# The old scores' bank booked one access at a time, attention's outputs loaded by pairs of token tiles, and a new list of due-time shifts, in a planned kernel of attention and a Fourier mix

## The chip, the cores and the metric

The kernel runs on one core of a Trainium2 chip. The metric is the device time of one execution in microseconds (us). Before the change it is 1681.3 us, the median of three runs (1677.09 to 1683.54).

The engines are TensorE (PE; PEld is its load of weights), VectorE (DVE), ScalarE (ACT) and GpSimd (POOL). SyncE (SP) issues the DMAs. PSUM, into which TensorE writes, is used in banks of 512 float32 numbers per partition.

## The reference

Two independent layers are computed and set side by side: attention over a window of 256 tokens (S = 2048, D = 1024, 32 heads of 32), and the real part of a two-dimensional Fourier transform, written as products with matrices.

```python
qkv = (x @ wqkv).reshape(B, S, 3, H, Dh)            # q, k, v by head
scores = einsum("bhqd,bhkd->bhqk", q, k) * Dh ** -0.5
mask = (i - j >= 0) & (i - j < 256)
p = softmax(where(mask, scores, -1e9))
a = einsum("bhqk,bhkd->bhqd", p, v) -> (B, S, D) @ wo

a_ = x @ dft_hid_re.T ; b_ = x @ dft_hid_im.T
b = dft_seq_re @ a_ - dft_seq_im @ b_
return concatenate([a, b], axis=-1)
```

## The kernel before

**Numbers.** Inputs are float32. Each operand is scaled by a power of two and split into a high and a low float16 part (ACT writes the high one, L503, L504 and L1201; DVE the low one, L508, L511 and L1202). A product is three TensorE passes: high by high, high by low, low by high (`PASSES`). The scale comes from the largest magnitude in the operand: a reduction (L529 on DVE, L1070 on ACT), a transpose of the column of maxima by TensorE into the bank `old` (L543, L1160), a reduction there (L545, L1162), and three tiny DVE instructions.

**Products.** Most large products take seven block products in place of eight (`seven`); the sums of blocks that this needs run on POOL and DVE (L1177). `seven` uses four PSUM banks `m`. Its first product is copied by ACT into a second bank as a start value (L1288), then accumulated into in both. Results are evacuated by ACT (L1379, L1572) and DVE (L1382, L1575).

**Stages.** To about 250 us: q, k and v. From there to about 1565 us attention runs block by block beside further products: the rest of q, k and v, then the Fourier layer, whose unit is `x` (the hidden transform) or `c` (the one along the sequence). Last come eight pairs of token tiles of the product with `wo`.

**A block of attention** is 128 queries of two heads. `s_step` writes the scores of the last two key tiles into a bank `s` and those of the third, oldest tile into one half of the bank `old` (L653). A DVE copy under a mask takes the old scores into the place of those above the diagonal (L664). DVE finds the maxima (L669), ACT the bias (L673) and the two exponentials, one for each head (L679). ACT and DVE split the result (L504, L508), a DMA transposes it (L688), POOL masks it (L694, L697). `v_step` multiplies two blocks by v into the one bank `pv` (L730), and DVE normalises (L735, L737, L741). `o_step` stores an output of four heads, transposed, in `ots`, by chunk of 512 tokens, group of four heads, part and token.

**The end.** `o_load` brings attention's outputs back, two loads for each pair of token tiles. `o_blocks` adds high and low parts (L1550), makes four sums (L1177), and splits them.

**What sets the order.** Nothing is issued as the Python code runs. `op` records every operation with its engine, an assumed duration, and what it reads and writes. `Plan.close` gives each a due time, counted back from TensorE's order of products. `Plan.run` moves due times: each entry of `SHIFTS` names a stretch of 20 us and a seed, and all operations due in that stretch are moved by pseudo-random amounts. `Plan.forward` then walks through time with the assumed durations: an engine that comes free takes the ready operation with the earliest due time. The order found there is written out as fixed instruction queues. On the chip each engine runs its queue in order and waits on semaphores. These waits follow from the tiles that instructions touch, whatever the plan assumed.

A `Ring` is a set of buffers used in turn. One with `free=True` gives a slot to whoever asks, once its last user is done. The bank `old` is such a ring with two slots, its two halves, shared by the old scores and the transposes of maxima.

Of the kernel before, what the change touches and what calls it, by code (L numbers as in the profile page):

```python
# [12 lines left out]
F16 = mybir.dt.float16  # L13
# [7 lines left out]
P = 128  # L21
# [64 lines left out]
class Ring:  # L86

    def __init__(self, plan, make, n, free=False):
        self.make, self.n, self.free, self.bufs, self.after = make, n, free, [], None
        plan.rings.append(self)  # L90
# [24 lines left out]
def scatter(n, seed):  # L115
# [6 lines left out]
SHIFTS = (  # L122
# [16 lines left out]
)  # L139


class Plan:
# [79 lines left out]
    def forward(self):  # L222
# [5 lines left out]
        held = {}  # L228
        gate = {}
        for ring in self.rings:  # L230
            if ring.free:
                for b in ring.bufs:
                    for o in b.heads:
                        gate.setdefault(o, []).append(b)
                    for o in b.ops:
                        held.setdefault(o, []).append(b)
                    b.todo, b.has = len(b.ops), False
# [16 lines left out]
        def start(o, t, e):  # L254
            nonlocal bus
            cost = o.cost
# [9 lines left out]
            if o.dma:  # L266
                bus = max(bus, fin - (BETWEEN if e == "SP" else 0.0)) + o.dma[0]
                fin = bus + o.dma[1]
                if e == "SP":
                    lanes.append(fin)  # L270
            fin += DRAIN if e == "PE" else SEM
            o.at, o.fin = t, fin
            order.append(o)
# [10 lines left out]
        def pick(e, t):  # L284
# [4 lines left out]
            while h:  # L289
# [6 lines left out]
                if any(not b.has and not room[b.ring] for b in gate.get(o, ())):  # L296
                    skipped.append(item)
                    continue
                got = o
                break  # L300
            for item in skipped:
                heapq.heappush(h, item)
            if got is not None and e == "DVE" and got.port:
                wait = lock["POOL"] - t - SHARED[e]
                if wait > 0.05:
                    skipped = []
                    while h and len(skipped) < 12:
                        item = heapq.heappop(h)
                        o = item[2]
                        skipped.append(item)  # L310
                        if not o.port and o.cost < wait + SLIP and not any(not b.has and not room[b.ring] for b in gate.get(o, ())):
                            skipped.pop()
                            skipped.append((got.due, got.n, got))
                            got = o
                            break
# [87 lines left out]
def fused_kernel(ctx: ExitStack, tc: tile.TileContext, xa, wqk, wv, xb, wd, cs, out):  # L403
# [56 lines left out]
    old_bank = ps_v.tile([P, 2, 2 * P], F32, name="old")  # L460
    old_ring = Ring(R, lambda k: old_bank[:, k], 2, free=True)
    s_ring = Ring(R, lambda k: ps_s.tile([P, 2, 2 * P], F32, tag="s", name=f"s_{k}"), 2)
# [77 lines left out]
    def scale_of(key, v, s, wk, down=2.0 ** -14, loose=False):  # L540
# [10 lines left out]

        dve(0.47, rest, w=[wk])

# [15 lines left out]
    def dkey(*a):  # L569
        return ("dram", *a)  # L570
# [25 lines left out]
    def attention():  # L596
# [33 lines left out]
        def s_step(b):  # L630
# [47 lines left out]
            for h in range(2):  # L678
                op("ACT", 0.32 + 0.00085 * w, lambda h=h: nc.scalar.activation(  # L679
                    sv()[:, h], sv()[:, h], AF.Exp, bias=bias.t[:, h:h + 1], scale=es),  # L680
                   r=[bias, ("esc", g // 2)], w=[(S, h)])
            hl = hl_ring.new()
# [468 lines left out]
    def u_look(n):  # L1151
# [18 lines left out]

        dve(0.7, rest, r=[("fa", p)], w=[v, f])
        su[n], fu[n] = v, f
# [361 lines left out]
    def o_load(q):  # L1534
        if q < NT // 2:
            for t in (2 * q, 2 * q + 1):
                b = os_[t] = raw_ring.new()
                load(lambda b=b: b.t.bitcast(F16).rearrange("p (g h t) -> p g h t", g=NG, h=2),
                     lambda t=t: ots[t // 4, :, :, :, t % 4 * P:t % 4 * P + P], 740, [b],
                     r=[dkey("o", t // 4, g) for g in range(NG)])  # L1540

    def o_blocks(q):
# [3 lines left out]
        r1, r2 = (y_ring if q == 0 else late_ring).new(), (y_ring if q == 0 else late_ring).new()  # L1546
        tv = lambda b: b.t.bitcast(F16).rearrange("p (g h t) -> p g h t", g=NG, h=2)
        ov = lambda b, h: b.t.bitcast(F16).rearrange("p (a g h t) -> p a g h t", a=2, h=2, t=P)[:, :, :, h]
        for r, o in ((r1, o1), (r2, o2)):
            dve(1.22, lambda r=r, o=o: nc.vector.tensor_tensor(r.t.rearrange("p a (g t) -> p a g t", t=P), ov(o, 0),  # L1550
                                                               ov(o, 1), op=ALU.add), r=[o], w=[(r, 0), (r, 1)],
                port=True)
        H_ = lambda r, a: (lambda: r.t[:, a])
        summed("DVE", H_(r1, 0), H_(r1, 0), H_(r2, 0), 512, [(r2, 0)], [(r1, 0)])
        summed("DVE", H_(r2, 0), H_(r2, 0), H_(r2, 1), 512, [(r2, 1)], [(r2, 0)], False)
        summed("DVE", H_(r2, 1), H_(r2, 1), H_(r1, 0), 512, [(r1, 0)], [(r2, 1)])
        summed("DVE", H_(r1, 1), H_(r1, 1), H_(r2, 1), 512, [(r2, 1)], [(r1, 1)])
        us = {}
        for r, pair in ((r2, (4, 2)), (r1, (1, 6))):
            x, y, ap = duo()  # L1560
# [3 lines left out]
            us[pair[0]], us[pair[1]] = position(x), position(y)  # L1564
        whole = lambda o, k: (lambda h, d: ((lambda: tv(o)[:, HG * k + d, h]), o))
        oq[q] = (whole(o1, 0), us[1], us[2], whole(o1, 1), us[4], whole(o2, 1), us[6])

    def pair_of_tiles(q, lhs, rhs, y1, y2, f, fk, out_y, hook, more=False, order=ORDER):
        half = lambda y, e: y.t[:, e] if len(y.t.shape) == 3 else y.t[:, e * CH:(e + 1) * CH]

        def copy(y, e, ps):
            op("ACT", 0.6, lambda: nc.scalar.activation(half(y, e), ps.t, AF.Copy, scale=f()), r=[ps, *fk], w=[(y, e)])  # L1572

# [182 lines left out]
```

## Time and profile before

| | us |
|---|---|
| median of three runs | 1681.3 |
| the profiled execution | 1678.3 |
| its span in the profile | 1676.4 |
| TensorE busy | 1647.7 |
| VectorE busy | 1400.5 |
| ScalarE busy | 1153.4 |
| GpSimd busy | 813.4 |

The profile is of one execution. "Idle before" a group of instructions is the time its engine stood still ahead of them, put down to the event that came last. Rows of products on TensorE overlap, since a product's row ends when its last result is written, well after the next has begun; so TensorE's busy time is the time in which any product is in flight. A list of waits has, for each pair of waiting and awaited lines, the total, the number of times and the longest. Rows of the timeline have the start, the time from the first start to the last end of the merged instructions, their count, and the idle time ahead.

### The profile page before, as it was taken

Reading aid. Unit: us, or ns where it says so; the run is one execution under the profiler, and the core shown is the slowest. Engines: PE = TensorE matmul, PEld = TensorE weight load, DVE = VectorE, ACT = ScalarE, POOL = GpSimd, SP = SyncE. Lnnn points to the kernel's source line nnn. Section 1 sums busy time; section 2 is a strip of 40 time slices with the busy share of each in tenths; the row PEclk is TensorE's granted clock in tenths of the full one; section 3 lists DMA queues with packets and bytes.
Section 4 is the critical chain, followed back from the end, with each engine's and each line's share of the span. In section 5 each row is a group of like instructions: output and inputs, shape, how many; then the busy total and the mean of one; then the engine's idle time right before and its main releaser. Section 6 shows DMA issues by size and latency. Waiting matters only on the chain.

```text
span 1676.4 us, 31757 instructions
## 1 busy us (share of the span) xinstructions
PE 1647.7 (98%) x11413; PEld 889.2 (53%) x11413; DVE 1400.5 (84%) x2376; ACT 1153.4 (69%) x1988; POOL 813.4 (49%) x797
## 2 busy tenths in 40 slices
PE   9999999999999999999999999999999999999999
PEld 4446787675444555555445545545555555554444
DVE  7989997667999998778999986898885799999651
ACT  6656636666987988977977766877665777775231
POOL 0233401323776954447956774754544476773100
PEclk9999999999999999999999999999999999999999
DMA  7389799979999889899899999789999779999732
GB/s 282 130 316 360 246 332 288 283 163 221 251 264 289 221 195 281 220 288 257 189 231 273 262 289 294 183 198 255 253 242 259 169 176 271 273 289 233 155 94 76
DMA packets 470302, 400.33 MB, mean 239 GB/s; under 512 B 342016, under 2 KB 397056, under 8 KB 470144
## 3 DMA queue, kind: packets, MB, share of 16 engines
q1 hardware_dynamic: 470144, 398.30, 90.0%
q8 instruction: 89, 1.46, 0.4%
q14 instruction: 69, 0.57, 0.1%
HBM read 215.37 MB, written 109.45 MB: 194 GB/s over the span
## 4 chain that ended last, share of the span: by engine, by line
PE 59%; DVE 17%; DMA 8%; ACT 7%; issue 6%; POOL 3%; SPq 0%; DVEq 0%; POOLq 0%; ACTq 0%
PE m L788 53%; DMA raw<-in_cs_dram 3%; DVE sth L1202 3%; DVE hl L508 3%; PE pv L730 3%; DMA t<-hl 2%; DVE mx L669 2%; PE s L653 2%; DVE s L664 2%; DVE ybig L1575 2%; ACT s L679 1%; ACT sth L1201 1%; ACT hl L504 1%; DVE reg L508 1%; POOL raw L1177 1%
## 5 line engine op out<-in xcount | busy, mean ns | idle before, releaser
L788 PE MATMUL m<-reg,sth 128*128 128x512 f16 x4992 | 1150.8, 379 | 10.8 <-DVE sth L1202 2.3
L788 PEld LDWEIGHTS <-sth 128*128 128x128 f16 x5748 | 544.7, 97 | 598.1 <-issue 12.3
L694 POOL TENSOR_SCALAR_AFFINE_SELECT z<-t 128x512 f16<-128x512 f16 x224 | 181.6, 821 | 373.9 <-PE pv L730 185.1
L1177 POOL TENSOR_TENSOR raw<-raw,raw 128x512 f32<-128x512 f32 x176 | 257.1, 1463 | 207.7 <-DVE sth L1202 164.7
L679 ACT ACTIVATE s<-s,bias,escs 128x256 f32<-128x256 f32 (+1 forms) x512 | 269.1, 528 | 12.3
L508 DVE TENSOR_TENSOR hl<-s,hl 128x512 f16<-128x512 f32 (+1 forms) x256 | 170.4, 668 | 65.0 <-ACT hl L504 62.4
L673 ACT ACTIVATE bias<-mx,pshift,escs 128x2 f32<-128x2 f32 x256 | 97.6, 383 | 159.4 <-DVE mx L669 158.7
L697 POOL TENSOR_SCALAR_AFFINE_SELECT t<-t 128x512 f16<-128x512 f16 x224 | 185.9, 841 | 5.3
L669 DVE TENSOR_REDUCE mx<-s 128x2 f32<-128x512 f32 (+1 forms) x256 | 169.0, 665 | 1.6
L1202 DVE SCALAR_TENSOR_TENSOR sth<-raw,sc,sth 128x1024 f16<-128x1024 f32 (+1 forms) x128 | 158.1, 1239 | 11.9 <-ACT sth L1201 11.5
L504 ACT ACTIVATE hl<-s 128x512 f16<-128x512 f32 (+1 forms) x256 | 147.5, 579 | 4.5 <-DMA t<-hl 1.4
L1201 ACT ACTIVATE sth<-raw,sc 128x1024 f16<-128x1024 f32 (+1 forms) x128 | 131.0, 1035 | 13.1 <-POOL raw L1177 6.5
L653 PEld LDWEIGHTS <-qk 96*128 96x128 f16 x1056 | 92.2, 98 | 83.5 <-issue 8.5
L1177 POOL TENSOR_TENSOR raw<-raw 128x512 f32<-128x512 f32 x80 | 119.9, 1500 | 31.3 <-DVE reg L511 20.9
L664 DVE COPY_PREDICATED s<-upper,old 128x256 f32<-128x256 uint32 x224 | 93.3, 420 | 19.7 <-PE s L653 8.8
L788 PE MATMUL m<-xz,sth 128*128 128x512 f16 x492 | 108.9, 379 | 0.0
L1070 ACT ACTIVATE junk<-raw 128x1024 uint8<-128x1024 f32 x82 | 86.5, 1054 | 25.4 <-DMA raw<-in_cs_dram 22.1
L730 PE MATMUL pv<-vt,t 128*128 128x65 f16 x1984 | 100.6, 185 | 0.0
L730 PEld LDWEIGHTS <-t 128*128 128x128 f16 x1984 | 89.1, 96 | 20.3 <-issue 8.8
L653 PE MATMUL s<-qk,qk 96*128 96x128 f16 (+1 forms) x608 | 94.5, 252 | 2.8 <-DVE hl L508 2.0
L730 PE MATMUL pv<-vt,z 128*128 128x65 f16 (+1 forms) x896 | 89.8, 185 | 5.5 <-DVE o L741 5.4
L1575 DVE SCALAR_TENSOR_TENSOR ybig<-m,fu,ybig 128x512 f32<-128x512 f32 x120 | 88.6, 741 | 5.7 <-PE m L788 4.9
(160 smaller groups left out, 2092.5 us busy)
## 6 DMA issues: line engine op xcount, KB each, us to landing
raw<-in_cs_dram SPq DMA_DIRECT2D x64, 512.0 KB, 5.7
raw<-in_wd_dram SPq DMA_DIRECT2D x48, 512.0 KB, 5.9
out_dram<-ybig SPq DMA_DIRECT2D x48, 512.0 KB, 5.8
ybig<-out_dram SPq DMA_DIRECT2D x36, 512.0 KB, 5.2
qs<-ybig SPq DMA_DIRECT2D x64, 256.0 KB, 4.0
raw<-in_xb_dram SPq DMA_DIRECT2D x32, 512.0 KB, 6.0
qk<-qs SPq DMA_DIRECT2D x64, 256.0 KB, 4.7
out_dram<-reg SPq DMA_DIRECT2D x30, 512.0 KB, 4.8
```

Source lines behind the costliest of these rows:

```text
L504: else nc.scalar.activation(dst(), src(), AF.Copy), r=r, w=w)
L508: op("DVE", c_dve(n), lambda: nc.vector.tensor_tensor(dst(), src(), hi(), op=ALU.subtract), r=r, w=w, port=port)
L653: nc.tensor.matmul(dst(j, a, e), qu.t[:, h, i * P:i * P + P], ku.t[:, h, ka:ke], start=True, stop=True, skip_group_check=True)
L669: dve(c_dve(2 * w), lambda: nc.vector.tensor_reduce(mx.t, sv(), axis=AX.X, op=ALU.max, negate=True), r=[(S, 0), (S, 1)], w=[mx])
L679: op("ACT", 0.32 + 0.00085 * w, lambda h=h: nc.scalar.activation(sv()[:, h], sv()[:, h], AF.Exp, bias=bias.t[:, h:h + 1], scale=es), r=[bi ...
L694: op("POOL", 0.637, lambda: nc.gpsimd.affine_select(out=z.t, in_=pk(), compare_op=ALU.is_gt, fill=0.0, base=0, pattern=[[0, 4], [-1, P]], ...
L697: op("POOL", 0.637, lambda: nc.gpsimd.affine_select(out=pk(), in_=pk(), compare_op=ALU.is_ge, fill=0.0, base=0, pattern=[[0, 4], [1, P]], ...
L730: nc.tensor.matmul(pvt()[:, r, j, lo:], lhs, vt.t[:, k % QB, at + lo:at + VW], start=a, stop=e, skip_group_check=True)
L788: nc.tensor.matmul(ps.t[:, j * n:j * n + n], lhs(), rhs(), start=first, stop=last, skip_group_check=True)
L1177: lambda: e.tensor_tensor(o(), a(), b(), op=ALU.subtract if sub else ALU.add), r=r, w=w, port=True)
L1201: op("ACT", c_act(n), lambda: nc.scalar.activation(dst(0), src(), AF.Copy, scale=scl()), r=[*r, sk_], w=wh)
L1202: op("DVE", c_dve(n, True), lambda: nc.vector.scalar_tensor_tensor(dst(1), src(), scl(), dst(0), op0=ALU.mult, op1=ALU.subtract), r=[*r, s ...
```

## The change

- `Ring` takes `alone`, and the ring of the bank `old` has it. While the plan is walked, an operation that touches this bank starts only after the one that touched it last has ended, whichever half either uses.
- The second exponential of a pair is recorded as reading the first one's result, so that it starts after it in the plan.
- Three assumed durations change: the end of a scale from 0.47 to 0.54 and from 0.7 to 0.64, ACT's copies of the last products from 0.6 to 0.64.
- `o_load` fetches, for a pair of token tiles, both tiles of four groups of heads in one load and both tiles of the other four in the next. Before, each load had one tile of all eight groups. `o_blocks` computes the same sums from the other layout, and splits them in the pairs (1, 4) and (6, 2) instead of (4, 2) and (1, 6).
- `SHIFTS` has other entries, and more of them.

No product, exponential or DMA is added or taken away. The lines of `fused_kernel` up to `o_blocks` have numbers 14 higher in the new code.

```diff
-    def __init__(self, plan, make, n, free=False):
+    def __init__(self, plan, make, n, free=False, alone=False):
...
 SHIFTS = (
-    (0, 52), (1, 373), (1, 443), (1, 507), (2, 804), (2, 928), (3, 1284), (3, 1388), (3, 1467),
+    (0, 73), (1, 382), (1, 468), (2, 749), (2, 858), (3, 1192), (4, 1393), (5, 1644), (5, 1834),
...
+        bank, banked = 0.0, {o for ring in self.rings if ring.alone for b in ring.bufs for o in b.ops}
...
+            if o in banked:
+                bank = fin
...
+                if o in banked and bank > t + 1e-9:
+                    skipped.append(item)
+                    put(bank, "free", o)
+                    continue
...
-    old_ring = Ring(R, lambda k: old_bank[:, k], 2, free=True)
+    old_ring = Ring(R, lambda k: old_bank[:, k], 2, free=True, alone=True)
...
-        dve(0.47, rest, w=[wk])
+        dve(0.54, rest, w=[wk])
...
-                   r=[bias, ("esc", g // 2)], w=[(S, h)])
+                   r=[bias, ("esc", g // 2), (S, 0)], w=[(S, h)])
...
     def o_load(q):
         if q < NT // 2:
-            for t in (2 * q, 2 * q + 1):
-                b = os_[t] = raw_ring.new()
-                load(lambda b=b: b.t.bitcast(F16).rearrange("p (g h t) -> p g h t", g=NG, h=2),
-                     lambda t=t: ots[t // 4, :, :, :, t % 4 * P:t % 4 * P + P], 740, [b],
-                     r=[dkey("o", t // 4, g) for g in range(NG)])
+            for a in range(2):
+                b = os_[2 * q + a] = raw_ring.new()
+                load(lambda b=b: b.t.bitcast(F16).rearrange("p (g h t) -> p g h t", g=HG, h=2),
+                     lambda a=a: ots[q // 2, :, HG * a:HG * a + HG, :, q % 2 * 2 * P:(q % 2 + 1) * 2 * P], 530, [b],
+                     r=[dkey("o", q // 2, HG * a + g) for g in range(HG)])
...
-        summed("DVE", H_(r1, 0), H_(r1, 0), H_(r2, 0), 512, [(r2, 0)], [(r1, 0)])
-        summed("DVE", H_(r2, 0), H_(r2, 0), H_(r2, 1), 512, [(r2, 1)], [(r2, 0)], False)
+        summed("DVE", H_(r1, 0), H_(r1, 0), H_(r1, 1), 512, [(r1, 1)], [(r1, 0)])
+        summed("DVE", H_(r1, 1), H_(r1, 1), H_(r2, 1), 512, [(r2, 1)], [(r1, 1)], False)
...
-        for r, pair in ((r2, (4, 2)), (r1, (1, 6))):
+        for r, pair in ((r1, (1, 4)), (r2, (6, 2))):
...
-            op("ACT", 0.6, lambda: nc.scalar.activation(half(y, e), ps.t, AF.Copy, scale=f()), r=[ps, *fk], w=[(y, e)])
+            op("ACT", 0.64, lambda: nc.scalar.activation(half(y, e), ps.t, AF.Copy, scale=f()), r=[ps, *fk], w=[(y, e)])
```

What this does to the queues is shown at three places.

TensorE at the start of the program, from the second half of the exact first products (L1421, in float32) to the first split product; `old` takes the maxima of x (`topone_169`) and of two weights. Before:

```order
L1421 MATMUL m_0_152<-reg_80,reg_78 128x512 x8
L1421 MATMUL m_0_173<-reg_80,reg_78 128x512 x2
L543 MATMUL old<-ident,topone_169 128x128
L1421 MATMUL m_0_173<-reg_80,reg_78 128x512 x4
L543 MATMUL old<-ident,topone_193 128x128
L543 MATMUL old<-ident,topone_176 128x128
L1421 MATMUL m_0_173<-reg_80,reg_78 128x512 x2
```

After (the maxima are `topone_167`, then `topone_179` and `topone_203`):

```order
L1435 MATMUL m_0_152<-reg_80,reg_78 128x512 x6
L557 MATMUL old<-ident,topone_167 128x128
L1435 MATMUL m_0_172<-reg_80,reg_78 128x512 x2
L557 MATMUL old<-ident,topone_179 128x128
L1435 MATMUL m_0_152<-reg_80,reg_78 128x512 x2
L1435 MATMUL m_0_172<-reg_80,reg_78 128x512 x2
L557 MATMUL old<-ident,topone_203 128x128
L1435 MATMUL m_0_172<-reg_80,reg_78 128x512 x4
```

The three transposes have moved apart and ahead: x's from behind ten exact products to behind six, the last weight's from behind fourteen to behind twelve.

DVE at the scale of the tenth unit of the Fourier layer (the transpose L1160 that the trace has at 824.74 us). `topone` is the column of maxima to be transposed, `sc` the scale made from it, `s` the scores of a block, `old` the bank. Before:

```order
L669 TENSOR_REDUCE mx_9992<-s_9920 128x2
L536 TENSOR_REDUCE topone_10011<-top_9975 128x1
L735 RECIPROCAL rs_10017<-pv 128x4
L508 TENSOR_TENSOR reg_78<-reg_78 128x2x512
L664 COPY_PREDICATED s_10008<-upper,old 128x2x128
L737 TENSOR_REDUCE pv<-pv 128x128
L508 TENSOR_TENSOR hl_10032<-s_9920,hl_10032 128x512
L669 TENSOR_REDUCE mx_10049<-s_10008 128x2
L1162 TENSOR_REDUCE sc_10054<-old 128x1
```

After:

```order
L678 COPY_PREDICATED s_10021<-upper,old 128x2x128
L522 TENSOR_TENSOR reg_78<-reg_78 128x2x512
L550 TENSOR_REDUCE topone_10052<-top_10009 128x1
L683 TENSOR_REDUCE mx_10055<-s_10021 128x2
L522 TENSOR_TENSOR hl_10044<-o_9523,hl_10044 128x512
L1589 SCALAR_TENSOR_TENSOR ybig<-m_42_9861,ybig 128x512
L678 COPY_PREDICATED s_10065<-upper,old 128x2x128
L522 TENSOR_TENSOR reg_78<-reg_78 128x512
L522 TENSOR_TENSOR hl_10094<-s_10021,hl_10094 128x512
L683 TENSOR_REDUCE mx_10104<-s_10065 128x2
L1176 TENSOR_REDUCE sc_10111<-old 128x1
```

The copy of the old scores stood three rows behind the column of maxima; it now stands two rows ahead of it, and the copy of the next block follows between the maxima and their scale.

DVE in the last stage, about 1584 us in the trace of before. `raw` are loads of attention's outputs, `m` a product's bank. Before:

```order
L1575 SCALAR_TENSOR_TENSOR reg_78<-m_77_19421,fo,reg_78 128x512
L508 TENSOR_TENSOR sth<-reg_78,sth 128x2x512 x2
L1550 TENSOR_TENSOR reg_78<-raw_19609 128x2x512
L1550 TENSOR_TENSOR reg_78<-raw_19579 128x2x512
L1177 TENSOR_TENSOR reg_78<-reg_78 128x512 x3
L1575 SCALAR_TENSOR_TENSOR reg_78<-m_75_19642,fo,reg_78 128x512
L1177 TENSOR_TENSOR reg_78<-reg_78 128x512
L508 TENSOR_TENSOR sth<-reg_78,sth 128x2x512
```

After:

```order
L1589 SCALAR_TENSOR_TENSOR reg_78<-m_77_19480,fo,reg_78 128x512
L522 TENSOR_TENSOR sth<-reg_78,sth 128x2x512
L1563 TENSOR_TENSOR reg_78<-raw_19612 128x2x512
L1563 TENSOR_TENSOR reg_78<-raw_19533 128x2x512
L1191 TENSOR_TENSOR reg_78<-reg_78 128x512 x3
L1589 SCALAR_TENSOR_TENSOR reg_78<-m_75_19642,fo,reg_78 128x512
L522 TENSOR_TENSOR sth<-reg_78,sth 128x2x512
L1191 TENSOR_TENSOR reg_78<-reg_78 128x512
```

The additions L1550 (now L1563) keep their place between the two evacuations; only the last of the four sums and the first split have changed places.

More of the change, by code (lines that the diff above doesn't have):

```diff
@@ L86 @@
 class Ring:
-    def __init__(self, plan, make, n, free=False):
-        self.make, self.n, self.free, self.bufs, self.after = make, n, free, [], None
+    def __init__(self, plan, make, n, free=False, alone=False):
+        self.make, self.n, self.free, self.alone, self.bufs, self.after = make, n, free, alone, [], None
         plan.rings.append(self)
@@ L254, in start @@
         def start(o, t, e):
-            nonlocal bus
+            nonlocal bus, bank
             cost = o.cost
@@ L310, in pick @@
                         skipped.append(item)
-                        if not o.port and o.cost < wait + SLIP and not any(not b.has and not room[b.ring] for b in gate.get(o, ())):
+                        if not o.port and o.cost < wait + SLIP and not (o in banked and bank > t + 1e-9) and not any(not b.has and not room[b.ring] for b in gate.get(o, ())):
                             skipped.pop()
@@ L1169, in rest @@
             nc.vector.tensor_scalar(f.t, fa[:, p:p + 1], vv, None, op0=ALU.mult)
-        dve(0.7, rest, r=[("fa", p)], w=[v, f])
+        dve(0.64, rest, r=[("fa", p)], w=[v, f])
         su[n], fu[n] = v, f
@@ L1546, in o_blocks @@
         r1, r2 = (y_ring if q == 0 else late_ring).new(), (y_ring if q == 0 else late_ring).new()
-        tv = lambda b: b.t.bitcast(F16).rearrange("p (g h t) -> p g h t", g=NG, h=2)
-        ov = lambda b, h: b.t.bitcast(F16).rearrange("p (a g h t) -> p a g h t", a=2, h=2, t=P)[:, :, :, h]
+        tv = lambda b: b.t.bitcast(F16).rearrange("p (g h e t) -> p g h e t", g=HG, h=2, e=2)
         for r, o in ((r1, o1), (r2, o2)):
-            dve(1.22, lambda r=r, o=o: nc.vector.tensor_tensor(r.t.rearrange("p a (g t) -> p a g t", t=P), ov(o, 0),
-                                                               ov(o, 1), op=ALU.add), r=[o], w=[(r, 0), (r, 1)],
-                port=True)
+            dve(1.22, lambda r=r, o=o: nc.vector.tensor_tensor(r.t.rearrange("p e (g t) -> p e g t", t=P),
+                                                               tv(o)[:, :, 0].rearrange("p g e t -> p e g t"),
+                                                               tv(o)[:, :, 1].rearrange("p g e t -> p e g t"), op=ALU.add),
+                r=[o], w=[(r, 0), (r, 1)], port=True)
         H_ = lambda r, a: (lambda: r.t[:, a])
-        summed("DVE", H_(r1, 0), H_(r1, 0), H_(r2, 0), 512, [(r2, 0)], [(r1, 0)])
-        summed("DVE", H_(r2, 0), H_(r2, 0), H_(r2, 1), 512, [(r2, 1)], [(r2, 0)], False)
+        summed("DVE", H_(r1, 0), H_(r1, 0), H_(r1, 1), 512, [(r1, 1)], [(r1, 0)])
+        summed("DVE", H_(r1, 1), H_(r1, 1), H_(r2, 1), 512, [(r2, 1)], [(r1, 1)], False)
         summed("DVE", H_(r2, 1), H_(r2, 1), H_(r1, 0), 512, [(r1, 0)], [(r2, 1)])
-        summed("DVE", H_(r1, 1), H_(r1, 1), H_(r2, 1), 512, [(r2, 1)], [(r1, 1)])
+        summed("DVE", H_(r2, 0), H_(r2, 0), H_(r2, 1), 512, [(r2, 1)], [(r2, 0)])
         us = {}
-        for r, pair in ((r2, (4, 2)), (r1, (1, 6))):
+        for r, pair in ((r1, (1, 4)), (r2, (6, 2))):
             x, y, ap = duo()
@@ L1564, in o_blocks @@
             us[pair[0]], us[pair[1]] = position(x), position(y)
-        whole = lambda o, k: (lambda h, d: ((lambda: tv(o)[:, HG * k + d, h]), o))
-        oq[q] = (whole(o1, 0), us[1], us[2], whole(o1, 1), us[4], whole(o2, 1), us[6])
+        whole = lambda o, e: (lambda h, d: ((lambda: tv(o)[:, d, h, e]), o))
+        oq[q] = (whole(o1, 0), us[1], us[2], whole(o2, 0), us[4], whole(o2, 1), us[6])
     def pair_of_tiles(q, lhs, rhs, y1, y2, f, fk, out_y, hook, more=False, order=ORDER):
```

37 rows, old and new, of the table SHIFTS are left out of this document.

## The prediction

> **What bounds the kernel now.** I read the page first, its engine shares, then the windows, TensorE's own waits, and the end of the chain.
>
> ```profile
> PE 1647.7 (98%) x11413; PEld 889.2 (53%) x11413; DVE 1400.5 (84%) x2376; ACT 1153.4 (69%) x1988; POOL 813.4 (49%) x797
> L788 PE MATMUL m<-reg,sth 128*128 128x512 f16 x4992 | 1150.8, 379 | 10.8 <-DVE sth L1202 2.3
> 1585.64 87.23 PE m L788 x403
> ```
>
> TensorE (PE) is busy for 1647.7 of 1676.4 us, so 28.7 us are idle. A product's row lasts 379 ns, but 403 in a row take 87.23 us, 216 ns each: rows overlap by 163 ns, so every visible wait behind such a product hides another 0.16 us. The change neither adds nor removes a product, and the granted clock is 1.00 in every stretch below. What it can win is therefore the idle 28.7 us and what is hidden at its edges; what it can lose has no such bound.
>
> The windows (core 0: stretch, its length, then busy time of PE, PEld, DVE, ACT, POOL, clock, DMA share, GB/s) say where the idle time lies:
>
> ```profile
> 0.00:240.00 240.00, 237.60 (x1402) 140.61 (x1403) 216.66 (x279) 141.69 (x183) 66.91 (x67) 1.00 0.77 276
> 240.00:400.00 160.00, 159.85 (x1417) 113.63 (x1416) 112.11 (x215) 98.89 (x194) 33.96 (x62) 1.00 0.98 246
> 400.00:560.00 160.00, 153.64 (x1087) 78.30 (x1084) 152.88 (x247) 136.00 (x246) 112.37 (x96) 1.00 1.04 266
> 560.00:800.00 240.00, 237.38 (x1643) 121.02 (x1642) 203.98 (x369) 201.45 (x362) 136.95 (x129) 1.00 0.93 242
> 800.00:1000.00 200.00, 194.70 (x1365) 99.13 (x1362) 187.94 (x346) 155.50 (x274) 141.34 (x126) 1.00 1.00 246
> 1000.00:1080.00 80.00, 79.80 (x584) 41.52 (x583) 60.35 (x112) 57.97 (x112) 43.64 (x44) 1.00 1.05 264
> 1080.00:1200.00 120.00, 115.29 (x828) 59.78 (x827) 106.73 (x200) 85.61 (x150) 68.42 (x71) 1.00 0.90 218
> 1200.00:1520.00 320.00, 318.00 (x2301) 164.87 (x2299) 276.31 (x503) 226.18 (x403) 194.53 (x190) 1.00 0.98 241
> 1520.00:1600.00 80.00, 78.61 (x473) 37.57 (x472) 62.51 (x88) 31.84 (x46) 15.28 (x16) 1.00 0.76 183
> ```
>
> Three crowded stretches (400 to 560, 800 to 1000, 1080 to 1200) lose 6.36 + 5.30 + 4.71 = 16.4 us in 480; the calm ones from 560 to 1520 lose 2.62 + 0.20 + 2.00 = 4.8 us in 640. Who ends these waits is in TensorE's own list (total us, times, longest):
>
> ```profile
> PE pv L730 <- DVE o L741: 5.4, 8, 2.0
> ...
> PE s L653 <- DVE hl L508: 2.0, 4, 1.1
> PE old L1160 <- DVE s L664: 1.9, 3, 1.5
> PE m L788 <- ACT m L1288: 1.7, 4, 0.9
> ...
> PE m L788 <- ACT reg L1379: 1.1, 1, 1.1
> PE m L788 <- DVE reg L1550: 1.1, 1, 1.1
> PE old L653 <- DVE s L664: 1.0, 4, 0.5
> ...
> PE old L653 <- DVE sc L1162: 0.7, 3, 0.3
> ```
>
> No resource is short on average; TensorE waits wherever the written order promised a result sooner than it came.
>
> **Part 1, the old scores' bank.** `old` has two halves in one bank. The waits show that a write into one half is held until a read of the other has ended:
>
> ```profile
> 821.08 0.38 PE L653 MATMUL s<-qk,qk 96*128 96x256 f16 x2
> 821.30 1.89 PE L788 MATMUL m<-reg,sth 128*128 128x512 f16 x8
> 824.74 0.32 PE L1160 MATMUL old<-ident,topone 128*128 128x128 f32 x1 [1.54 <-DVE s L664]
> ...
> 824.26 0.41 DVE L664 COPY_PREDICATED s<-upper,old 128x256 f32<-128x256 uint32 x1
> ```
>
> The transpose of a column maximum needs nothing of that copy, yet waits 1.54 us for it. All such waits in the list are 1.9 + 1.0 + 0.7 = 3.6 us in 10 cases, with 10 x 0.16 hidden 5.2. The old plan did not know this rule, the new one books it. The order shows the effect: writes that wait for a read of the other half fall from 26 to 12. Those with less than 1.3 us of products between the read's own producer and the write (a 0.42 us copy and two handovers barely fit) fall from 9 to 0. Writes that wait for the same half go from 108 to 116. At the place above, the copy now stands two rows ahead of the maximum, and the next copy's write comes later. I take 4.2 of the 5.2 us as won, the rest being same-half waits. Bounds: nothing won; all 5.2; or a loss of 2.6 us if held scores arrive too late for their own readers (the `s L653` waits, 2.0 + 4 x 0.16, doubled).
>
> **Part 2, the paired exponentials.** In the program the second already followed the first on the same queue:
>
> ```profile
> 499.91 1.10 ACT L679 ACTIVATE s<-s,bias,escs 128x256 f32<-128x256 f32 x2
> 19.89 2.19 ACT L503 ACTIVATE sth<-reg,scw 128x1024 f16<-128x1024 f32 x2 [0.43 <-DVE scw L550]
> L679 ACT ACTIVATE s<-s,bias,escs 128x256 f32<-128x256 f32 x480 | 255.5, 534 | 11.4
> L503 ACT ACTIVATE sth<-reg,scw 128x1024 f16<-128x1024 f32 x6 | 6.7, 1143 | 2.7 <-DVE scw L550 2.3 <-PE m L788 0.3
> ```
>
> Two conversions of 1.143 us take 2.19, an overlap of 0.10; two exponentials of 0.534 take 1.10, no overlap but a gap of 0.03. So the added dependency costs the chip nothing; it lets the plan see 0.1 us per pair that ACT really needs, and with the copies' longer cost it will promise less. What hangs on ACT's lateness is `s L653 <- hl L508`: 2.6 us with its hidden part. I take a third, 0.8 us; bounds 0 to 2.6, or as much lost.
>
> The Trainium skill (ScalarE: Activation LUTs, "What ACT_TABLE_LOAD costs") has back-to-back ACTIVATEs overlapping by about 93 ns. The conversions agree, the exponentials on this bank do not. By that rule the new dependency would take 93 ns of overlap from 256 pairs, an estimate of 24 us of ACT, and this part's 0.8 us would be lost, not won, so the sum would be 1.6 us worse; by the rows nothing is taken.
>
> **Part 3, the new list.** It reorders all engines. What the order lets me price:
>
> ```profile
> 21.09 0.60 PE L788 MATMUL m<-reg,sth 128*128 128x512 f16 x2 [0.42 <-ACT sth L503]
> 22.42 1.90 PE L788 MATMUL m<-reg,sth 128*128 128x512 f16 x8 [0.72 <-DVE sth L511]
> ```
>
> The start: the last weight's maximum is transposed ahead of four exact products, not two, and x's scale ahead of ten, not six. ACT reaches that weight after three conversions of x, as before, but these can start earlier. Of the 0.42 + 0.72 us I take 0.7 as won (bounds 0 to 1.1 plus 0.3 hidden; a loss of 0.4 if the earlier transpose waits for its reductions).
>
> The `pv` bank: pairs of pv steps with under 3 us of other work between them fall from 23 to 17. A quarter of 5.4 + 8 x 0.16 = 6.7 us is 1.7 (bounds -2 to 6.7: the eight waits may move).
>
> ACT's handoffs, against the change: a product's bank that ACT must copy and free with under 1 us of other products meanwhile occurs 24 times instead of 14.
>
> ```profile
> L1288 ACT ACTIVATE m<-m 128x512 f32<-128x512 f32 x77 | 44.8, 582 | 36.7 <-PE m L788 35.1 <-DVE ybig L511 1.5
> L1201 ACT ACTIVATE sth<-raw,sc 128x1024 f16<-128x1024 f32 x96 | 109.1, 1142 | 13.0 <-POOL raw L1177 6.5 <-DVE sc L1168 3.6 <-PE m L788 1.9
> ```
>
> Eleven of the 24 lie before 250 us, where three did and cost nothing visible: from 0 to 240 TensorE's 2.40 us are 1.26 ahead of the first product and the 0.42 + 0.72 above. At 0.1 us of hidden cost the eight more there make 0.8. Three, not one, leave only 0.1 to 0.2 us for a 0.58 us copy: two more at 0.5 make 1.0. Together 1.8 lost; bounds 0 and 10 x 1.14 = 11.4, when each finds a 1.142 us conversion ahead of it on ACT.
>
> **Part 4, the outputs of attention.** A load keeps its 512 KB, in rows of 512 instead of 256 bytes; two sums and two splits trade places. After 1600 us nothing here is waited for, since TensorE runs to its last product from 1585.64. What remains is in 1520 to 1600: 1.39 us idle. Of that 1.10 is this:
>
> ```profile
> 1584.36 1.24 DVE reg L1550
> ...
> 1585.64 1.02 PE L788 MATMUL m<-reg,sth 128*128 128x512 f16 x4 [1.10 <-DVE reg L1550]
> ...
> raw<-ots SPq DMA_DIRECT2D x16, 512.0 KB, 5.4
> ```
>
> In the new order the same addition stands between the same two products, so it stays. A landing takes 5.4 us now; shorter ones could only end waits inside what is left. I take the other 0.3 us as won; bounds -1.1 (a second such wait: one more addition is waited for by TensorE in the new order) to 1.4.
>
> **The sum.** -4.2 - 0.8 - 0.7 - 1.7 + 1.8 - 0.3 = -5.9 us. The profiled execution took 1678.3 (span 1676.4 and 1.9 around it), 3.0 below the median of 1681.3. So 1672.4 for such an execution, and 1675.4 against the median, 0.35% less. A measurement of this kernel can tell about 0.5%, 8.4 us, from no change.
>
> **Rivals.**
> - *The new list also calms the crowded stretches*, because a plan that sees the real waits spreads its work: then those 480 us lose at the calm rate, 4.8 / 640, that is 3.6 instead of 16.4, and with the start 13.5 us are won: 1667.8. For it: from 1200 to 1520 DVE is at 86% and TensorE loses little. Against it: DVE is at 94 to 96% in the first two crowded ones, and no order lessens that.
> - *The change doesn't do what it says*: bank waits come back at other places, because DVE reaches the copies late, as the 1.88 us addition ahead of the copy at 824.26 made it; then only 1.7 us of the sum remain: 1679.6.
> - *Slower, by ACT's handoffs*: each of the ten new ones finds a conversion of 1.142 us ahead of it, and nothing else is won: 1681.3 + 11.4 = 1692.7. It decides from about seven such hits on. For it: the plan places them with no slack. Against it: ACT is 59% busy to 240 us and the three of before cost nothing there.
>
> **How the numbers follow.** Forecast 0.45 (spread about 5 us, so 0.10 of it passes the 8.4 us), the calm list 0.33, no effect 0.14, slower 0.08. Faster by over 0.5%: 0.10 + 0.31 = 0.41. Slower by over 0.5%: 0.08 and a little of the others, 0.10. Within: 0.49. The range runs from 1664, which leaves out a quarter of the calm case, to 1686, which leaves out the slower case.
>
> **What would show it.** Right: TensorE's list has under 1.5 us of waits of `old` for a copy or maximum, the start's two waits sum to under 0.6 us, the wait at the L1550 addition is still about 1.1 us, and PE's idle total is near 23 us. Wrong: waits of products for the copies L1288 and L1379 (numbers 14 higher in the new code) of over 6 us, or an idle total above 28. Under 17 speaks for the calm list. If the exponential pairs take longer than 1.10 us, the page's overlap was there after all.

## The result and the profile after

The changed kernel takes 1669.6 us, the median of six runs (1667.07 to 1672.77), beside 1679.3 us for the kernel before, measured with it (six runs, 1677.09 to 1683.54). The ratio is 0.9938, with a 95% interval of 0.9925 to 0.9951: 9.7 us less, where 5.9 were forecast. The profiled execution took 1668.2 us, its span is 1666.2. Of two experiments below (the changed kernel's first one without a list, and no dependency of the exponentials with a fresh list) the profiled execution ran at a granted clock of 0.56 and 0.65 and is left out of their times, while one run at 0.97 stays in the 1708.3 us of the kernel before with a fresh list, which would be 1705.3 without it.

The first row is the page's engine shares of the kernel after, then follow the windows, with the columns as before.

```profile
PE 1644.5 (99%) x11413; PEld 889.0 (53%) x11413; DVE 1398.6 (84%) x2376; ACT 1148.1 (69%) x1988; POOL 804.9 (48%) x797
```

```profile
0.00:240.00 240.00, 238.47 (x1406) 141.00 (x1407) 215.36 (x276) 142.01 (x184) 68.09 (x67) 1.00 0.77 271
240.00:400.00 160.00, 159.98 (x1426) 114.05 (x1424) 117.67 (x224) 99.53 (x200) 36.24 (x64) 1.00 1.03 260
400.00:560.00 160.00, 156.24 (x1085) 79.11 (x1084) 152.33 (x247) 134.63 (x244) 116.03 (x98) 1.00 1.03 262
560.00:800.00 240.00, 238.82 (x1661) 122.40 (x1659) 201.59 (x369) 200.03 (x365) 136.38 (x129) 1.00 0.96 246
800.00:1000.00 200.00, 197.34 (x1402) 102.13 (x1401) 196.15 (x355) 156.85 (x277) 141.94 (x127) 1.00 0.96 249
1000.00:1080.00 80.00, 78.35 (x576) 40.48 (x575) 58.51 (x110) 60.19 (x112) 43.79 (x46) 1.00 0.98 246
1080.00:1200.00 120.00, 118.24 (x844) 60.80 (x843) 105.48 (x205) 86.61 (x152) 60.85 (x67) 1.00 0.95 238
1200.00:1520.00 320.00, 316.15 (x2315) 164.59 (x2313) 280.25 (x505) 224.44 (x399) 191.83 (x194) 1.00 0.99 244
1520.00:1600.00 80.00, 78.30 (x425) 36.34 (x424) 52.89 (x71) 28.24 (x41) 9.75 (x9) 1.00 0.57 149
```

The idle total of TensorE fell from 28.7 to 1666.2 - 1644.5 = 21.7 us. The span fell by more, 10.2 us: busy time fell too, by 3.2. Fewer waits hide less at their edges: TensorE's whole list has 46 waits before and 27 after, and 19 x 0.16 are 3.0. The three crowded stretches lose 3.76 + 2.66 + 1.76 = 8.2 us, half of the 16.4 before. The calm ones from 560 to 1520 lose 1.18 + 1.65 + 3.85 = 6.7, where it was 4.8. So half of the crowded loss is gone, and about 2 us came back in the calm stretches. (The stretches are fixed in time; the new kernel is up to some 12 us further in its products, so their contents are not quite the same.)

From TensorE's list of waits after the change (total us, times, longest):

```profile
PE m L802 <- ACT m L1302: 3.9, 3, 1.9
PE pv L744 <- DVE o L755: 2.1, 4, 0.9
PE m L802 <- DVE sth L1216: 1.4, 2, 0.9
...
PE m L802 <- DMA sth<-xhs: 1.2, 1, 1.2
PE m L802 <- DVE reg L1563: 1.1, 1, 1.1
PE m L802 <- ACT reg L1393: 1.0, 2, 0.8
PE old L667 <- DVE sc L1176: 0.6, 1, 0.6
PE old L1174 <- DVE s L678: 0.5, 1, 0.5
...
PE old L667 <- DVE s L678: 0.5, 1, 0.5
...
PE s L667 <- DVE hl L522: 0.5, 2, 0.3
...
PE m L802 <- DVE ybig L1589: 0.3, 1, 0.3
```

Waits of `old` for a copy or a maximum are 1.6 us in 3 cases, not 3.6 in 10. Those for an output of attention (`pv`) fell from 5.4 to 2.1, those for a split of scores (`s`) from 2.0 to 0.5, those for evacuations of the Fourier layer (`ybig`) from 2.2 to 0.3. Waits for ACT's copies (L1302, L1393) rose from 2.8 to 4.9, of which 3.4 lie in two places:

```profile
831.68 2.95 PE L802 MATMUL m<-reg,sth 128*128 128x512 f16 x12 [1.89 <-ACT m L1302]
...
1511.65 1.02 PE L802 MATMUL m<-reg,raw 128*128 128x512 f16 x4 [1.52 <-ACT m L1302]
```

### The profile page after: what moved, and what is told of

It is laid out like the page before. It is cut to its first block, busy times and chain, and to the rows that moved or that the text cites. A ratio compares the mean times of both kernels' runs of the same rounds, so it can differ in the third digit from the quotient of the medians.

```text
span 1666.2 us, 31741 instructions
## 1 busy us (share of the span) xinstructions
PE 1644.5 (99%) x11413; PEld 889.0 (53%) x11413; DVE 1398.6 (84%) x2376; ACT 1148.1 (69%) x1988; POOL 804.9 (48%) x797
## 4 chain that ended last, share of the span: by engine, by line
PE 68%; DVE 14%; DMA 6%; issue 4%; ACT 4%; POOL 2%; SPq 1%; DVEq 0%; POOLq 0%; ACTq 0%
PE m L802 60%; PE pv L744 3%; DVE sth L1216 2%; DMA t<-hl 2%; PE s L667 2%; DVE hl L522 2%; DVE mx L683 2%; DVE reg L522 1%; POOL raw L1191 1%; DMA raw<-in_cs_dram 1%; DVE s L678 1%; DVE ybig L1589 1%; PE old L667 1%; ACT sth L1215 1%; PE m L1435 1%
## 5 line engine op out<-in xcount | busy, mean ns | idle before, releaser
L1191 POOL TENSOR_TENSOR raw<-raw,raw 128x512 f32<-128x512 f32 x176 | 248.6, 1414 | 252.6 <-DVE sth L1216 214.2
L1216 DVE SCALAR_TENSOR_TENSOR sth<-raw,sc,sth 128x1024 f16<-128x1024 f32 (+1 forms) x128 | 162.3, 1273 | 14.6 <-ACT sth L1215 13.5
L1191 POOL TENSOR_TENSOR raw<-raw 128x512 f32<-128x512 f32 x80 | 119.9, 1501 | 18.8 <-DVE reg L525 10.2
```

The source lines that it names most:

```text
L1191: lambda: e.tensor_tensor(o(), a(), b(), op=ALU.subtract if sub else ALU.add), r=r, w=w, port=True)
L1216: op("DVE", c_dve(n, True), lambda: nc.vector.scalar_tensor_tensor(dst(1), src(), scl(), dst(0), op0=ALU.mult, op1=ALU.subtract), r=[*r, s ...
```

## The experiments

Two theories were on trial. **A: what the plan now knows** (the bank, the exponentials) makes an order that the chip can keep. **B: the list**: `SHIFTS` is another list of pseudo-random moves, and the order that it gives happens to be better. (The new list has 202 entries, the old one 136; nothing here shows how either was found.) Each time below stands beside runs of the kernel before on the same chip, whose medians were 1677.9 to 1679.4 us.

### Both kernels without a list

```diff
-SHIFTS = (
...
-)
+SHIFTS = ()
```

The kernel before:

> The kernel before with an empty list of shifts. Theory A (the plan's knowledge of the bank is what pays): slower than before by 10 us or more, since the list only tuned the plan, and 4 to 6 us of it in waits of `old` for a copy L664 or a reduction L1162 as before. Theory B (the new list alone pays, by being longer): slower than before too, and as long as the changed kernel with an empty list, within 2 us.

The changed kernel, twice:

> The changed kernel with an empty list of shifts. Theory A: 4 us or more faster than the kernel before with an empty list, with under 2 us of waits of `old` for a copy or a reduction. Theory B: within 2 us of it.

> The changed kernel without its list, once more, for a profile that can be read. Theory A (the plan knows the bank's rule, so its order has the copies and maxima of `old` in time): the waits of `old` for a copy or a maximum sum to under 2.2 us, about half of the 4.2 us that the old kernel without a list has; time 1700 us as in the first run, within 5. Theory B (the list alone made the difference): the waits of `old` are as in the old kernel without a list, 4 us or more.

Measured: 1712.4 us before (ratio 1.0197, interval 1.0166 to 1.0228) and 1699.2 and 1698.8 after (1.0122, 1.0098 to 1.0146; 1.0116, 1.0096 to 1.0135). The waits of `old` for a copy or a maximum, in TensorE's list of the kernel before without a list (its lines have numbers 17 lower), and below it of the changed one (24 lower than with its list):

```profile
PE old L1143 <- DVE s L647: 2.3, 2, 1.5
...
PE old L636 <- DVE s L647: 1.6, 4, 0.5
...
PE old L636 <- DVE sc L1145: 0.3, 1, 0.3
```

```profile
PE old L1150 <- DVE s L654: 2.1, 3, 0.9
```

The waits are 4.2 and 2.1 us, about as theory A had them, and the changed plan is 13 us faster with no list at all. But a list alone is worth 29 to 33 us to each plan, far more than that (the granted clock of the runs without one, 0.995 to 0.999 for 1.000, can make some 5 us of it, an estimate from 0.3% of 1650 us), so the next question is how much of the 13 us is the chance of one order.

### Without a list, one part of the plan's knowledge taken back

```diff
-    old_ring = Ring(R, lambda k: old_bank[:, k], 2, free=True, alone=True)
+    old_ring = Ring(R, lambda k: old_bank[:, k], 2, free=True)
```

> The changed kernel without its list and without the booking of the bank `old`; the exponentials' dependency stays. Theory A: slower than the changed kernel without a list by 3 to 6 us (1704 to 1707 us), and the waits of `old` for a copy or a maximum come back to 4 us or so. Theory B: no difference beyond 3 us in time. If the bank counts for all of the 11.8 us between the two kernels without lists, 1712 us.

```diff
-                   r=[bias, ("esc", g // 2), (S, 0)], w=[(S, h)])
+                   r=[bias, ("esc", g // 2)], w=[(S, h)])
```

> The changed kernel without its list and without the dependency of the second exponential on the first; the bank's booking stays. By the prediction (0.8 us for this part, which sets nothing on the chip): within 2 us of the changed kernel without a list. If the exponentials' booking is the greater part of the 11.8 us: slower by 6 us or more, with more waits of scores for the split behind the exponentials.

Measured: 1702.4 us without the bank's booking, 1704.5 without the exponentials', beside 1698.8 with both: 3.7 and 5.7 us slower. The first difference isn't clear of the spread (four runs each, 1698.1 to 1706.4 beside 1695.9 to 1701.6), the second is. Taken alone this would give the exponentials the larger share. But waits for splits of scores, which were to grow without the exponentials' booking, are 5.2 us there and 8.8 with both. The waits of `old` speak against so simple a reading as well. Without the bank's booking, then without the exponentials':

```profile
PE old L1150 <- DVE s L654: 4.2, 5, 1.6
```

```profile
PE old L1150 <- DVE s L654: 3.0, 3, 1.6
...
PE old L643 <- DVE s L654: 2.0, 1, 2.0
```

The kernel that still books the bank has 5.0 us of such waits, the one that does not has 4.2. The plan keeps the bank's accesses apart in its own time only. That the copies come later on the chip than planned is the likely reason for waits in spite of it; planned and measured times were not compared.

### Lists found anew, by one search for all

For four plans a list was found by the same search, stretch by stretch, out of a hundred shifts for each: the kernel before, the changed kernel, and the changed kernel with one or the other line above taken back. The lists have 426 to 474 entries; the changed kernel's begins so:

```diff
 SHIFTS = (
-    (0, 73), (1, 382), (1, 468), (2, 749), (2, 858), (3, 1192), (4, 1393), (5, 1644), (5, 1834),
...
+    (0, 200012), (0, 200017), (0, 200021), (0, 200037), (0, 200041), (0, 200046), (0, 200081), (1, 200109), (1, 200199),
...
```

> The kernel before with a list found anew for its plan by the same search as the next three kernels use (the same number of tries for each stretch of 20 us). Theory A (what the plan knows decides): slower than the next kernel by 8 to 14 us, about 1682 us, with the waits of `old` for a copy or a maximum over 3 us. Theory B (the length and luck of the list decide): within 4 us of the next one.

> The changed kernel with a list found anew by that search. Theory A: about 1670 us, as the changed kernel with its own list, waits of `old` for a copy or a maximum under 2 us. Theory B: as the kernel before with its fresh list, within 4 us.

> The changed kernel without the booking of the bank, with a list found by that search. By the prediction the bank is the largest term (4.2 us): about 1674 us and waits of `old` for a copy or a maximum over 3 us. By the kernels without lists it is worth 2.7 us: about 1672.5. If the bank counts for nothing, within 1.5 us of the changed kernel with a fresh list.

> The changed kernel without the dependency between the exponentials, with a list found by that search. By the prediction (0.8 us): about 1671 us. By the kernels without lists (5 us, the larger part): about 1675 us or more, with more waits for splits and for ACT behind the exponentials.

| list | before | changed | changed, bank not booked | changed, exponentials not booked |
|---|---|---|---|---|
| its own | 1679.3 | 1669.6 | | |
| none | 1712.4 | 1699.2, 1698.8 | 1702.4 | 1704.5 |
| fresh | 1708.3 | 1693.9 | 1682.1 | 1691.4 |

The changed plan beats the old one with each kind of list, by 9.7, 13 and 14.5 us (11.4 from the 1705.3). Its parts don't hold up: without the bank's booking the fresh list gives 1682.1 us (ratio to before 1.0018, 1.0008 to 1.0028), 11.8 us *faster* than with it, and without the exponentials' 2.4 us faster, which three runs from 1689.4 to 1699.6 can't tell from nothing. Both were expected slower than the changed kernel with its fresh list. The levels of the first three were missed, too, by 26, 24 and 8 us. In the kernel before with a fresh list the waits of `old` are 7.7 us in 14 cases, as theory A had it (over 3). But the changed kernel with its fresh list books the bank, and where under 2 us were expected it has these waits:

```profile
PE old L693 <- DVE s L704: 3.1, 4, 1.3
PE old L1200 <- DVE s L704: 1.9, 4, 0.7
```

That is 5.0 us in 8 cases; without the booking it is 2.0 in 5:

```profile
PE old L692 <- DVE s L703: 2.0, 5, 0.6
```

So one plan moves by 29 us with its list (1669.6 to about 1699). The search recovers only 4 to 7 of them: with the fresh list each plan is 24 to 29 us slower than with its own. And with two lists of equal make a part can look like a gain or a loss of several us. What a single part of the plan's knowledge is worth can't be read from such runs. Three pairs of the same sign speak for the whole of theory A, but with lists that differ by so much chance isn't excluded, and for the pair with their own lists a better list isn't excluded either.

### The bank's waits taken out of the kernel before, its order kept

This experiment needs no list. In the order of the kernel before, at eleven places where a write into `old` waited for a read on DVE, the instruction ahead of that read is moved behind it.

```diff
     placed = R.run()
+    for late, soon in ((1402, 1410), (1783, 1888), (3056, 3061), (4069, 4196), (4351, 4429), (5056, 5071), (5848, 5856),
+                       (6420, 6304), (6299, 6304), (6570, 6587), (7310, 7387), (7210, 7606)):
+        o = R.ops[late]
+        placed.remove(o)
+        placed.insert(placed.index(R.ops[soon]) + 1, o)
```

> The kernel before in its own order, except that at eleven places where a write into `old` waited for a read of it on DVE, that read is moved ahead of the DVE instruction that stood in front of it (of two, at one place). Nothing else is moved on any engine. Between the starts of TensorE's products these eleven places cost 5.0 us (1.7 of them at 824.74). Prediction's bank term: such waits fall from 3.6 us to about 1 in TensorE's list and the time falls by 4 to 5 us, to about 1674.5. Rival, the waits turn up later (TensorE reaches the next late result sooner): waits of `old` fall all the same, but others grow, and less than 2 us is won.

Measured: 1678.5 us beside 1679.3 (12 and 17 runs), ratio 0.9995, interval 0.9981 to 1.0008, that is from 3.2 us won to 1.3 lost. The 4 to 5 us are excluded, and the rival holds. From TensorE's list of this kernel:

```profile
PE pv L730 <- DVE o L741: 3.9, 7, 1.0
PE m L788 <- DVE ybig L1575: 3.7, 6, 0.9
PE s L653 <- DVE hl L508: 3.1, 3, 2.3
...
PE old L653 <- DVE sc L1162: 0.6, 2, 0.3
...
PE old L1160 <- DVE s L664: 0.2, 1, 0.2
```

Waits of `old` fell from 3.6 us in 10 cases to 0.8 in 3. Those for `ybig` and for splits rose from 2.2 + 2.0 to 3.7 + 3.1, by 2.6 us. Others fell (`pv` from 5.4 to 3.9), so TensorE's idle total is 26.8 us, 1.9 less than before; but its busy time rose from 1647.7 to 1649.2, and the span of the profiled execution fell by only 0.4. The place of the longest wait shows how one such gain is lost. TensorE in this kernel (the transpose of the maxima is the row of `topone`):

```profile
822.17 1.89 PE L788 MATMUL m<-reg,sth 128*128 128x512 f16 x8
823.90 0.27 PE L1160 MATMUL old<-ident,topone 128*128 128x128 f32 x1
...
825.31 2.75 PE L788 MATMUL m<-reg,sth 128*128 128x512 f16 x12 [0.27 <-ACT ybig L1572]
...
830.45 1.89 PE L788 MATMUL m<-reg,sth 128*128 128x512 f16 x8 [0.75 <-DVE ybig L1575]
```

In the kernel before, the same rows of products start at 821.30, 825.76 and 830.00, the transpose at 824.74. This kernel begins the place 0.87 us later and starts the transpose, which no longer waits 1.54 us, 0.84 earlier: 1.7 us gained. But the next products wait 0.27 us for ACT and 0.75 for DVE's evacuation L1575, and at 830.45 TensorE is 0.45 us late again: 1.3 of the 1.7 are lost within 7 us. DVE, first in the kernel before, then with the copy moved ahead:

```profile
820.83 0.68 DVE L669 TENSOR_REDUCE mx<-s 128x2 f32<-128x512 f32 x1
...
822.30 0.15 DVE L536 TENSOR_REDUCE topone<-top 128x1 f32<-128x2 f32 x1 [0.79 <-ACT junk L1070]
...
822.46 1.88 DVE L508 TENSOR_TENSOR reg<-reg 128x1024 f16<-128x1024 f32 x1
...
826.33 0.92 DVE L508 TENSOR_TENSOR hl<-o,hl 128x512 f16<-128x512 f32 x1
...
828.85 0.68 DVE L1575 SCALAR_TENSOR_TENSOR ybig<-m,ybig 128x512 f32<-128x512 f32 x1
```

```profile
821.69 0.68 DVE L669 TENSOR_REDUCE mx<-s 128x2 f32<-128x512 f32 x1
...
822.75 0.15 DVE L536 TENSOR_REDUCE topone<-top 128x1 f32<-128x2 f32 x1 [0.39 <-ACT junk L1070]
...
822.91 0.41 DVE L664 COPY_PREDICATED s<-upper,old 128x256 f32<-128x256 uint32 x1
823.23 1.99 DVE L508 TENSOR_TENSOR reg<-reg 128x1024 f16<-128x1024 f32 x1
...
826.87 1.25 DVE L508 TENSOR_TENSOR hl<-o,hl 128x512 f16<-128x512 f32 x1
...
829.72 0.68 DVE L1575 SCALAR_TENSOR_TENSOR ybig<-m,ybig 128x512 f32<-128x512 f32 x1
```

From the maxima to the evacuation DVE takes 8.02 us in the one and 8.03 in the other: it has the same instructions to do in either order. The idle time at the maxima's column is 0.40 us less (0.39 for 0.79), but two instructions run longer, from 1.88 to 1.99 and from 0.92 to 1.25 us; why isn't shown. TensorE comes earlier and waits there. At this place DVE sets the pace, and the wait for it can't be saved by itself.

### The end: loads and buffers

The changed kernel with `o_load` and `o_blocks` as before, all else kept (both functions replaced by the old text):

```diff
-            for a in range(2):
-                b = os_[2 * q + a] = raw_ring.new()
...
+            for t in (2 * q, 2 * q + 1):
+                b = os_[t] = raw_ring.new()
...
```

> The changed kernel with the loads and sums of attention's outputs as before, the new list kept. If the new loads cost something where they begin (TensorE waits for raw<-ots in the profile after, 0.64 and 1.68 us later than without, near 1502 and 1512), this is 1 to 2.5 us faster than the changed kernel, some 1667.5. If the loads are worth nothing either way: 1669.6 within 1.5. If they were part of the gain: 1671 or more.

The changed kernel with the late sums' buffers apart from the cells of `wo`, so that the addition no longer lies inside the range of addresses that the products read. Of the edit the buffers are shown; in the last stage the cells move to the other half of a slot, with their loads and reads:

```diff
-    late_ring = Ring(R, lambda k: tsum[:, LSLOT[k % 6], :, :2].rearrange("p h k c -> p h (k c)").bitcast(F32), 6)
+    late_ring = Ring(R, lambda k: tsum[:, LSLOT[k % 6], 0].rearrange("p (a k) c -> p a (k c)", a=2).bitcast(F32), 6)
...
```

> The changed kernel, with the sums' buffers of the last stage in one contiguous half of a slot and the weights' cells in the other half, so that the addition L1563 and the products no longer touch interleaved stretches of one slot. If the wait of 1.1 us at that addition is only for the overlap of the two ranges and not for data, it is gone and the kernel ends 1.2 us earlier (1668.4). If it is for data, the wait stays at 1.1 us.

Measured: 1667.7 us (ratio 0.9938, 0.9918 to 0.9957) and 1669.1 us (0.9943, 0.9921 to 0.9964), both as the changed kernel. The first is the level that was expected if the new loads cost something, but its ratio to the kernel before is that of the changed kernel, 0.9938, so the new layout of the loads gives or costs nothing that can be measured. In the trace, from 1480 to 1600 us, TensorE has two waits with the old loads, 0.59 us for a load and 0.33 for an addition; in the changed kernel they are 0.47, 1.52, 0.60 and 1.10, but the order there differs in more than the loads. In the second the wait at the addition is gone from TensorE's list and its products run on without it, so it was for the overlap of the two ranges and not for data (the changed kernel, then the one with the buffers apart):

```profile
1575.38 1.02 PE L802 MATMUL m<-reg,sth 128*128 128x512 f16 x4 [1.10 <-DVE reg L1563]
```

```profile
1572.04 4.70 PE L802 MATMUL m<-reg,sth 128*128 128x512 f16 x21
```

The 1.1 us don't show in the median, whose runs spread over 5 us; the span of the profiled execution is 1666.5 us, no less than 1666.2. No version measured beats the changed kernel by more than the runs can tell.

## Why the prediction was right, and where it was not

The range held the time, and the sign was right; the gain was 3.8 us larger than forecast. The forecast of 1675.4 rests on 1681.3, a median of three runs. From the 1679.3 that were measured with the result it is 1673.4, and the rival of the calm list 1665.8: the 1669.6 lie 3.8 us from either. Step by step:

- **The bank.** The waits fell, from 3.6 to 1.6 us (just over the 1.5 that was named), with what hides at their edges from 5.2 to 2.1. The step that failed is "I take 4.2 of the 5.2 us as won, the rest being same-half waits": it prices a wait that goes at its full length. In the kernel before, the same kind of waits were taken out with nothing else moved, 5.0 us between the starts of products, and 0.85 us of median were won, with an interval that includes none. That belongs to the lower bound, "nothing won", and to the question what is late next: at 825.31 and 830.45 it was the evacuations.
- **The exponentials.** Waits for splits fell by 1.5 us in 2 cases less, 1.8 with the hidden part, where 0.8 was taken; but this isn't this part's own gain, since without a list its booking was worth 5.7 us and with fresh lists -2.4. Pairs in one go still take as long as before, 1.09 to 1.11 us, so the booking costs the chip nothing. The Trainium skill's overlap of ACTIVATEs (ScalarE: Activation LUTs, "What ACT_TABLE_LOAD costs") isn't there for them with or without it:

```profile
504.52 1.09 ACT L693 ACTIVATE s<-s,bias,escs 128x256 f32<-128x256 f32 x2
...
517.94 1.11 ACT L693 ACTIVATE s<-s,bias,escs 128x256 f32<-128x256 f32 x2
```

- **The start.** Both waits are gone from TensorE's rows, and the idle time to 240 us fell from 2.40 to 1.53; 0.7 was taken.
- **The `pv` bank.** From 6.7 us with the hidden part to 2.1 + 4 x 0.16 = 2.7: 4.0 went, where a quarter, 1.7, was taken. This is the term that was sized worst.
- **ACT's handoffs.** From 2.8 to 4.9 visible us: 2.1 lost, 1.8 taken. The size agrees by luck in part. The sum put 0.8 us, at 0.1 each, on handoffs before 250 us, where the list has one wait of 0.20. No run shows the 0.1. The loss is mostly the two waits of 1.89 and 1.52 us at 831.68 and 1511.65, where the copy stands behind other work of ACT: behind a row of conversions and splits at the first, at the second behind a split that waits 4.72 us for DVE. Whether these are the two handoffs that were priced at 0.5 isn't shown.
- **The end.** The wait at the addition stayed at 1.1 us, as said. But the 0.3 us taken as won didn't come: from 1520 to 1600 TensorE is idle for 0.60 + 1.10 us, where it was 1.39.
- **Not in the sum:** waits for evacuations and conversions on DVE (L1575, L1202 before), 2.2 + 0.7 + 2.3 us, are 0.3 + 1.4 after. Against that stand new waits of kinds that the list of before doesn't have, 3.6 us in 6 cases, the longest 1.2 us for the DMA `sth<-xhs`.

Idle time and hidden edges together fell by the 10.2 us of the span, because many kinds of waits fell at once. That is in part the rival **the calm list**: the crowded stretches lose 8.2 us, midway between their 16.4 and the 3.6 of the calm rate. By the prediction's own sign it isn't that rival in full: the idle total is 21.7, near the 23 of the forecast and not under 17. The objection to the rival was wrong, though. "DVE is at 94 to 96% in the first two crowded ones, and no order lessens that": the two stretches show two ways round it.

Ahead of the first, an order can do DVE's work earlier. From 240 to 400 us, where TensorE hardly waits, DVE is busy for 117.67 us after the change and was for 112.11 before. The kernel with only the bank's waits taken out, whose order there is nearly that of before, has

```profile
240.00:400.00 160.00, 159.91 (x1411) 113.76 (x1409) 113.22 (x216) 98.67 (x193) 33.98 (x62) 1.00 1.00 248
```

113.22 us: about 1 us is a matter of what falls inside the window's edges, and some 4 us of DVE's work are done earlier by the new order. Counted by TensorE's products instead of time it is 3.7 us, and at the product that the kernel before begins at 560 us the head start is used up.

Into the second, from 800 to 1000 us, DVE brings no head start. When 3888 of the 7380 products of L788 have begun (at 800 us before, 794 after), it has been busy for 685.8 us before and for 681.1 after, so it has done less. Yet TensorE loses 2.66 us in that stretch instead of 5.30, with DVE busy for 196.15 of the 200 us instead of 187.94. A DVE at 94% still stood idle for 12 us; now it is 4, so here the order inside the stretch is the better one. This is read from the traces; no run moved that work alone. Which of the plan's new rules, if any, led to it stays open: the lists' own spread hides it.

## What to carry to other kernels

A wait that the profile charges to one pair of instructions is worth its length only if nothing behind it is late as well (here eleven such waits, 5.0 us, gave 0.85): before pricing it, see what the awaited engine does next and whether it has idle time there. Where a search or pseudo-random numbers decide an order, one run with and without a rule tells nothing of the rule: either keep the order and move only the instructions in question, or compare many orders of each kind. An engine that is nearly full in a stretch isn't the end of what an order can win: look for work that can be done ahead of the stretch, and for the idle time that the engine still has inside it.

## What was not expected of the hardware

Two kernels with the same 11413 products differ in TensorE's busy time: 1644.5 us in the changed kernel, and here the kernel before with a fresh list:

```profile
PE 1660.2 (97%) x11413; PEld 889.2 (52%) x11413; DVE 1400.4 (82%) x2376; ACT 1158.9 (68%) x1988; POOL 815.3 (48%) x797
```

Busy time is the union of overlapping rows, so a wait shorter than the overlap of 0.16 us, and that much of every longer one, counts as busy; idle time understates what waits cost. The trace of 1660.2 us has a mean granted clock of 0.998 beside 1.000; as an estimate, 0.2% of 1650 us, that can make 3 of the 15.7 us between the two, not all. And loads of attention's outputs land in the same time with rows of 512 bytes (the changed kernel) and of 256 (with the old loads), a median of 4.7 us; the row is the same in both:

```profile
raw<-ots SPq DMA_DIRECT2D x16, 512.0 KB, 4.7
```

The 5.4 us of the kernel before were thus not a matter of the rows' length; with its fresh list they are 4.5, with 256 bytes too.
